# Loading the third tile of x through GpSimd's queue instead of SyncE's

## The chip, the cores and the metric

The kernel runs on one core of a Trainium2 chip. The metric is the device time of one execution in microseconds (us), the median of several runs. Beside it there is one profiled execution, whose trace gives every instruction's start and duration from the first instruction on; its span is the time from the first to the last instruction.

## What is computed

The input is a sequence of 2048 tokens with 512 features, in bf16. It is normalised, then put through a linear-attention block with 32 heads of 16 features and through a gated feed-forward block of width 1792; both results and the input are added.

```
def _A_ref(x, wqkv, w_phi, wo):
    ...
    pq = jnp.einsum("bhsd,hdf->bhsf", q, w_phi)
    pk = jnp.einsum("bhsd,hdf->bhsf", k, w_phi)
    phi_q = jnp.concatenate([_softmax(pq, axis=-1), _softmax(-pq, axis=-1)], axis=-1)
    phi_k = jnp.concatenate([_softmax(pk, axis=-1), _softmax(-pk, axis=-1)], axis=-1)
    kv = jnp.einsum("bhsf,bhsd->bhfd", phi_k, v)
    z  = jnp.einsum("bhsf->bhf", phi_k)
    num = jnp.einsum("bhqf,bhfd->bhqd", phi_q, kv)
    den = jnp.einsum("bhqf,bhf->bhq", phi_q, z)[..., None] + 1e-6
    o = num / den
    ...
def _B_ref(x, w_gate, w_up, w_down):
    g = jnp.einsum("bsd,df->bsf", x, w_gate)
    u = jnp.einsum("bsd,df->bsf", x, w_up)
    h = g * u
    return jnp.einsum("bsf,fd->bsd", h, w_down)
x = A_x
xn = _layernorm(x, axis=-1)
return x + _A_ref(xn, A_wqkv, A_w_phi, A_wo) + _B_ref(xn, B_w_gate, B_w_up, B_w_down)
```

## The kernel before

Tokens are cut into 16 tiles of 128 rows (`NT`), grouped by four (`GT`); a tile of x is 128 x 512 bf16, 128 KB, and lies in `xall[:, n, :]`. It is called x0 to x15 here. Features are cut into four chunks of 128 (`DC`). `xnT` holds the normalised x with the features on the partitions, as matmuls need it.

All weights stay in SBUF. They and x are fetched at the start by a list of DMAs, most of them issued by SyncE one after another (lines 82 to 95): x0, x2, the v part of `wqkv` in two halves (`wv`, L75), then the first columns of the gate and up weights (`wg`, `wu`, L72), `wphi` (L87), more of `wg` and `wu`, the transposed load of the k part (`wT2`, which the trace calls wT, L89), x4 to x7, the rest of `wg` and `wu`, x8 to x15, `wd` and `wo`. x1 and x3 are issued by ScalarE (lines 102 and 103). The issue of every x load stands in the helper `dma_x`, so that it has line 69 in the trace, whichever queue it goes to. GpSimd issues no DMA.

From line 98 on the order of each engine's instructions is that in which they are written (`manual_schedule`). What stands ahead of that line is only the DMAs of SyncE.

The opening treats the first four tiles apart, since nothing else can run before they are in. For a tile n:

- the rows are summed into `tots[n]`: x0 and x3 by VectorE (`sum_of`, L373), x1 and x2 by ScalarE (L377, which writes the scaled copy `junk` and takes the sum from the accumulator);
- VectorE subtracts the sum from 512 times x (`sub_sum`, L337) into `xns[n]`; the missing factor 1/std is put in later, where the results of matmuls are read;
- TensorE transposes the four chunks with the identity `ident` into PSUM (`lt`, L205), and ScalarE, for half of x0 VectorE, copies them to `xnT` (L206);
- TensorE multiplies with `wv` (`first_v` through `proj`, L236), the two first chunks of features for x0, x1 and x2, then the others; the results for x0 and x1 lie in the banks called kv, those of x2 and x3 in banks called pv.

The written order on ScalarE is: sum of x1, sum of x2, then the copies of the transposes. On VectorE: sum of x0, centring of x0 in two halves, centring of x1, copy of half of x0's transposes, centring of x2, sum of x3, centring of x3, then the statistics of all four (L153). On TensorE: eleven warm-up matmuls on a constant (L308; ten before everything else, one after the transposes of x1), transposes of x0 and x1, transposes of x2, v matmuls for x0, x1 and x2, transposes of x3, more v matmuls, then gate and up matmuls (`ffn`, L274 and L278).

GpSimd first makes the constants: `ident` (through `make_identity`, which the trace shows under masks.py:197 and 199), and `BO`, a block mask (L116, L110, L112). Later it computes 1/std (L345, L347), the block diagonal `bd` from `BO` and `wphi` (L212) and, in the main part, the products of the feature maps.

Behind the opening a long part follows in which TensorE goes from one matmul to the next: gate and up matmuls interleaved with the k and v projections of the remaining tiles, then attention and the output matmuls (`fin`, L290 and L293) with the stores.

Of the kernel before, what the change touches and what calls it, by code (L numbers as in the profile page):

```python
# [8 lines left out]
BF16 = mybir.dt.bfloat16  # L9
F32 = mybir.dt.float32  # L10
AF = mybir.ActivationFunctionType
# [10 lines left out]
def kernel(  # L22
# [12 lines left out]
    nc = tc.nc  # L35
    P = 128
    S, D = A_x.shape[-2], A_x.shape[-1]
# [4 lines left out]
    DC = D // P  # L42
# [10 lines left out]
    consts = ctx.enter_context(tc.tile_pool(name="consts", bufs=1))  # L53
# [4 lines left out]
    wv = wpool.tile([P, DC, D], BF16)  # L58
# [9 lines left out]
    def dma_x(lo, hi, eng=nc.sync):  # L68
        eng.dma_start(out=xall[:, lo:hi, :], in_=x_view[:, lo:hi, :])
# [1 line left out]
    def dma_cols(eng, w, src, lo, hi, at=0):  # L71
        eng.dma_start(out=w[:, :, lo - at:hi - at], in_=src[:, lo:hi].rearrange("(c p) f -> p c f", p=P))  # L72

    def dma_wv(lo, hi):
        nc.sync.dma_start(out=wv[:, lo:hi, :],  # L75
                          in_=A_wqkv[lo * P:hi * P, 2 * D:3 * D].rearrange("(c p) f -> p c f", p=P))

    def dma_gu(lo, hi):
        dma_cols(nc.sync, wg, B_w_gate, lo, hi)
        dma_cols(nc.sync, wu, B_w_up, lo, hi)  # L80

    dma_x(0, 1)
    dma_x(2, 3)
    dma_wv(0, 2)
    dma_wv(2, DC)
    dma_gu(0, 2 * P)
    nc.sync.dma_start(out=wphi[:], in_=A_w_phi.rearrange("(c h) d f -> (h d) c f", c=DC))  # L87
    dma_gu(2 * P, 5 * P)
# [5 lines left out]
    nc.sync.dma_start(out=wd[:], in_=B_w_down.rearrange("(c p) d -> p c d", p=P))  # L94
    nc.sync.dma_start(out=wo[:], in_=A_wo.rearrange("(c p) n -> p c n", p=P))

    ET = mybir.EngineType
    ctx.enter_context(tc.manual_schedule(engines={ET.PE, ET.DVE, ET.Activation, ET.Pool, ET.SP}))
    ones = nc.const_aps.tensor(1.0, [P, P], BF16)
    first = consts.tile([P, 1], BF16)  # L100
    nc.scalar.activation(out=first[:], in_=ones[:, 0:1], func=AF.Exp, scale=1.0)
    dma_x(1, 2, nc.scalar)
    dma_x(3, 4, nc.scalar)
    ident = consts.tile([P, P], BF16)
    make_identity(nc, ident[:])
    mhalf = consts.tile([P, GT], F32)
# [416 lines left out]
```

## Time and profile before

| what | us |
|---|---|
| median of 3 runs (lowest, highest) | 220.69 (220.66, 221.0) |
| the profiled execution | 220.62 |
| its span, first to last instruction | 218.9 |
| the two x issues of SyncE, from 0.79 | 0.87 |
| the two x issues of ScalarE, from 0.85 | 0.86 |
| the two wv issues of SyncE, from 1.71 | 0.94 |
| sum of x0 on VectorE starts | 3.36 |
| sum of x1 on ScalarE starts | 3.61 |
| sum of x2 on ScalarE starts | 4.37 |
| transposes of x2 on TensorE start | 5.55 |
| first v matmul starts | 5.79 |

The engines are called PE (TensorE's matmuls), PEld (its weight loads), DVE (VectorE), ACT (ScalarE), POOL (GpSimd) and SP (SyncE); SPq and ACTq are the queues in which they issue DMAs. L69 is line 69 of the kernel; an arrow in a row points from what is read to what is written. The chain of waits is followed back from the last instruction to what released each step. The time that a DMA takes stands as "us to landing", from the start of its issue; it can be several times the duration of the issue itself, which is what a queue's row in the timeline shows. The granted clock of TensorE is 1.0 over the whole span.

### The profile page before, as it was taken

The numbers are of one execution on the slowest core, as the hardware profiler recorded it, in microseconds if no ns is written. First come the engines' busy times: TensorE is split into PE (matmuls) and PEld (weight loads), VectorE is DVE, ScalarE is ACT, GpSimd is POOL, SyncE is SP. The second block draws the span as 40 slices with busy tenths as digits, with TensorE's granted clock in tenths as the row PEclk, the third lists the DMA queues.
The fourth block names the chain that finished last, engine by engine and source line by source line (L and its number), as shares of the span: only waits on it lengthen the run. The fifth ranks groups of instructions, "written<-read, shape, count | busy, mean of one in ns | idle before, by whom it ended". The sixth has DMA issues, their size and how long they took to land.

```text
span 218.9 us, 3494 instructions
## 1 busy us (share of the span) xinstructions
PE 214.9 (98%) x1293; PEld 103.1 (47%) x1293; DVE 140.6 (64%) x239; ACT 89.8 (41%) x160; POOL 74.1 (34%) x71
## 2 busy tenths in 40 slices
PE   7999999999999999999999999999999999999994
PEld 3444445454444444444544444444444444454443
DVE  4868867886598758576599773296655655454321
ACT  6645686569575875565435212141231322100000
POOL 2540843363358554636045333033123033000000
PEclk9999999999999999999999999999999999999999
DMA  6999996003202540202028455114441431612301
GB/s 200 273 301 374 372 235 111 15 0 51 48 0 49 51 91 5 48 3 48 1 41 103 77 114 114 39 24 96 96 75 24 95 72 27 97 48 72 75 24 48
DMA packets 48529, 19.91 MB, mean 91 GB/s; under 512 B 37504, under 2 KB 48512, under 8 KB 48512
## 3 DMA queue, kind: packets, MB, share of 16 engines
q1 hardware_dynamic: 48224, 19.42, 39.7%
q10 hardware_dynamic: 288, 0.26, 0.3%
q8 instruction: 10, 0.16, 0.3%
q14 instruction: 7, 0.06, 0.1%
HBM read 8.67 MB, written 2.10 MB: 49 GB/s over the span
## 4 chain that ended last, share of the span: by engine, by line
PE 96%; DMA 1%; ACT 1%; DVE 0%; issue 0%
PE g L274 22%; PE fin L290 22%; PE u L278 22%; PE fin L293 6%; PE k L236 6%; PE q L236 6%; PE pv L236 6%; PE kv L330 2%; PE ab L462 2%; DMA xall<-in_A_x_dram 1%; PE kv L236 1%; ACT junk L377 1%; PE pq L225 1%; PE tp L205 0%; DVE xn L337 0%; DVE o_sb L300 0%
## 5 line engine op out<-in xcount | busy, mean ns | idle before, releaser
L274 PE MATMUL g<-xnT,wg 128*128 128x512 bf16 x224 | 57.5, 379 | 0.0
L278 PE MATMUL u<-xnT,wu 128*128 128x512 bf16 x224 | 57.5, 379 | 0.0
L282 DVE TENSOR_TENSOR hT<-u,g_sb 128x512 bf16<-128x512 f32 x56 | 37.0, 667 | 24.3 <-PE u L278 16.2
L253 POOL TENSOR_TENSOR phiq<-e,rsum 128x1024 bf16<-128x1024 f32 x16 | 30.9, 1933 | 63.5 <-DVE rsum L251 56.0
L281 ACT CAST g_sb<-g 128x512 bf16<-128x512 f32 x56 | 32.9, 587 | 47.1 <-PE g L274 46.9
L249 DVE TENSOR_REDUCE sums<-e 128x64 f32<-128x1024 f32 x32 | 38.9, 1216 | 20.1 <-ACT e L246 20.1
L290 PE MATMUL fin<-wd,hT 128*128 128x512 bf16 (+2 forms) x238 | 51.1, 366 | 0.0
L253 POOL TENSOR_TENSOR phik<-e,rsum 128x1024 bf16<-128x1024 f32 x16 | 30.9, 1932 | 40.0 <-DVE rsum L251 37.9
L278 PEld LDWEIGHTS <-wu 128*128 128x128 bf16 x224 | 21.9, 98 | 26.4
L290 PEld LDWEIGHTS <-hT 128*128 128x128 bf16 x238 | 22.5, 98 | 24.7
L274 PEld LDWEIGHTS <-wg 128*128 128x128 bf16 x224 | 21.1, 98 | 24.0
L236 PEld LDWEIGHTS <-xnT 128*128 128x128 bf16 x192 | 17.5, 98 | 18.3 <-ACT xnT L206 0.3
L300 DVE TENSOR_TENSOR o_sb<-fin,xall 128x512 bf16<-128x512 f32 (+2 forms) x13 | 8.5, 651 | 20.5 <-PE fin L293 20.5
L251 DVE RECIPROCAL rsum<-sums 128x64 f32<-128x64 f32 x32 | 17.7, 553 | 3.1
L293 PE MATMUL fin<-wo,oT 128*128 128x512 bf16 (+2 forms) x68 | 16.6, 366 | 0.0
L236 PE MATMUL k<-W1k,xnT 128*128 128x512 bf16 x64 | 16.4, 379 | 0.0
L236 PE MATMUL q<-W1q,xnT 128*128 128x512 bf16 x64 | 16.4, 378 | 0.0
L245 ACT ACTIVATE e<-q 128x512 f32<-128x512 f32 x12 | 7.2, 597 | 22.2 <-PE q L236 22.2
L236 PE MATMUL pv<-wv,xnT 128*128 128x512 bf16 x56 | 14.4, 379 | 0.0
L475 DVE TENSOR_TENSOR otok<-ab,rden 128x512 bf16<-128x512 f32 x16 | 11.1, 692 | 0.6
L322 ACT CAST vt<-pv 128x512 bf16<-128x512 f32 x12 | 7.0, 587 | 10.0 <-PE pv L236 10.0
L153 DVE BATCH_NORM_STATS2 stats<-xall 128x6 f32<-128x512 bf16 x16 | 10.6, 665 | 0.0
(62 smaller groups left out, 130.6 us busy)
## 6 DMA issues: line engine op xcount, KB each, us to landing
out_dram<-o_sb SPq DMA_DIRECT2D x15, 128.0 KB, 2.0
wd<-in_B_w_down_dram SPq DMA_DIRECT2D x1, 1792.0 KB, 15.5
xall<-in_A_x_dram SPq DMA_DIRECT2D x1, 1024.0 KB, 11.4
wg<-in_B_w_gate_dram SPq DMA_DIRECT2D x1, 640.0 KB, 8.5
wu<-in_B_w_up_dram SPq DMA_DIRECT2D x1, 640.0 KB, 9.7
wv<-in_A_wqkv_dram SPq DMA_DIRECT2D x2, 256.0 KB, 4.1
xall<-in_A_x_dram SPq DMA_DIRECT2D x1, 512.0 KB, 4.3
wg<-in_B_w_gate_dram SPq DMA_DIRECT2D x1, 512.0 KB, 5.2
```

The source lines that it names most:

```text
L153: nc.vector.bn_stats(out=stats[:], in_=xall[:, n, :])
L236: nc.tensor.matmul(ps, lhsT=xnT[:, j, n * P:(n + 1) * P], rhs=w[:, j, :], start=(j == 0), stop=(j == DC - 1))
L249: nc.vector.tensor_reduce(out=sums[:], in_=ev, axis=AX.X, op=ALU.add)
L251: nc.vector.reciprocal(out=rsum[:].rearrange("p a b -> p (a b)"), in_=sums[:])
L253: nc.gpsimd.tensor_tensor(out=phi[:].rearrange("p g (x f) -> p (g x) f", f=DH), in0=ev, in1=rsum[:].to_broadcast((P, 2 * H, DH)), op=ALU.mult)
L274: nc.tensor.matmul(gps, lhsT=wg[:, c, f * P:(f + 1) * P], rhs=xnT[:, c, T * TT:(T + 1) * TT], start=(c == 0), stop=(c == DC - 1))
L278: nc.tensor.matmul(ups, lhsT=wu[:, c, f * P:(f + 1) * P], rhs=xnT[:, c, T * TT:(T + 1) * TT], start=(c == 0), stop=(c == DC - 1))
L281: nc.scalar.copy(out=g_sb[:], in_=gps)
L282: nc.vector.tensor_tensor(out=hTs[T][:, f, :], in0=ups, in1=g_sb[:], op=ALU.mult)
L290: nc.tensor.matmul(ps, lhsT=hTs[T][:, f, t4 * P:(t4 + 1) * P], rhs=wd[:, f, lo:lo + w], start=(f == 0), stop=False)
L293: nc.tensor.matmul(ps, lhsT=oTs[n][:, c, :], rhs=wo[:, c, lo:lo + w], start=False, stop=(c == DC - 1))
L475: nc.vector.tensor_tensor(out=o_tok[:].rearrange("p (b h d) -> p b h d", b=2, d=DH), in0=abv[:, :, :, 0:DH], in1=rden[:].to_broadcast((P, ...
```

## The change

x2 goes to GpSimd's queue; SyncE issues x0 and then wv in its two halves, followed by the unchanged rest of its list; ScalarE issues x1 and x3 as before. In the text the block with `manual_schedule`, the first activation and ScalarE's two loads moves up ahead of SyncE's remaining DMAs, so that these now stand behind the line from which the written order is kept. GpSimd's load of x2 stands ahead of `make_identity` and `BO`, so it is GpSimd's first instruction behind the four small constants that every program starts with. `dma_wv` takes the issuing engine as an argument, and gets SyncE both times.

```
-    def dma_wv(lo, hi):
-        nc.sync.dma_start(out=wv[:, lo:hi, :],
-                          in_=A_wqkv[lo * P:hi * P, 2 * D:3 * D].rearrange("(c p) f -> p c f", p=P))
+    def dma_wv(lo, hi, eng):
+        eng.dma_start(out=wv[:, lo:hi, :],
+                      in_=A_wqkv[lo * P:hi * P, 2 * D:3 * D].rearrange("(c p) f -> p c f", p=P))
...
     dma_x(0, 1)
-    dma_x(2, 3)
-    dma_wv(0, 2)
-    dma_wv(2, DC)
+    dma_wv(0, 2, nc.sync)
+    dma_wv(2, DC, nc.sync)
+
+    ET = mybir.EngineType
+    ctx.enter_context(tc.manual_schedule(engines={ET.PE, ET.DVE, ET.Activation, ET.Pool, ET.SP}))
+    ones = nc.const_aps.tensor(1.0, [P, P], BF16)
+    first = consts.tile([P, 1], BF16)
+    nc.scalar.activation(out=first[:], in_=ones[:, 0:1], func=AF.Exp, scale=1.0)
+    dma_x(1, 2, nc.scalar)
+    dma_x(3, 4, nc.scalar)
+    dma_x(2, 3, nc.gpsimd)
     dma_gu(0, 2 * P)
     nc.sync.dma_start(out=wphi[:], in_=A_w_phi.rearrange("(c h) d f -> (h d) c f", c=DC))
     dma_gu(2 * P, 5 * P)
...
-    ET = mybir.EngineType
-    ctx.enter_context(tc.manual_schedule(engines={ET.PE, ET.DVE, ET.Activation, ET.Pool, ET.SP}))
-    ones = nc.const_aps.tensor(1.0, [P, P], BF16)
-    first = consts.tile([P, 1], BF16)
-    nc.scalar.activation(out=first[:], in_=ones[:, 0:1], func=AF.Exp, scale=1.0)
-    dma_x(1, 2, nc.scalar)
-    dma_x(3, 4, nc.scalar)
     ident = consts.tile([P, P], BF16)
     make_identity(nc, ident[:])
```

## The prediction

> **What bounds the kernel now.** First the busy shares and the chain that ended last.
>
> ```profile
> span 218.9 us, 3494 instructions
> ...
> PE 214.9 (98%) x1293; PEld 103.1 (47%) x1293; DVE 140.6 (64%) x239; ACT 89.8 (41%) x160; POOL 74.1 (34%) x71
> ...
> PE 96%; DMA 1%; ACT 1%; DVE 0%; issue 0%
> ```
>
> TensorE is busy for 214.9 of 218.9 us. The 4.0 us without it lie in three places by the timeline: 0.83 before its first warm-up matmul, 0.28 between the last of these (ends 4.14) and the first transpose at 4.42, and 2.86 after its last matmul (215.80 + 0.24 = 216.04), while the last tile is added and stored. From 4.42 to 216.04 TensorE has no hole. So a change of loads can move the end only through the first 5.6 us, and what it moves there is passed on whole: nothing later can absorb it. That stretch of the chain of waits reads:
>
> ```profile
> 0.85 2.74 DMA xall<-in_A_x_dram
> 3.59 0.02 issue
> 3.61 0.46 ACT junk L377
> 4.07 0.08 issue
> 4.15 0.19 ACT junk L377
> 4.34 0.02 issue
> 4.37 0.73 ACT junk L377 x2
> 5.10 0.05 issue
> 5.15 0.36 DVE xn L337
> 5.51 0.05 issue
> 5.55 0.40 PE tp L205 x4
> 5.95 0.86 PE kv L236 x4
> ```
>
> Columns are start, length, what. x1 (issued by ScalarE at 0.85) lands at 3.59; ScalarE sums its rows (L377) until 4.34, sums x2 from 4.37 to 5.10, VectorE centres x2 (L337), TensorE transposes it at 5.55, and the v matmuls follow without a hole. x2's load is not in this chain: ScalarE is not ready for it before 4.37. When it lands comes from the loads that were in flight at 1.17 and at 1.27 us.
>
> ```profile
> xall<-in_A_x_dram SPq DMA_DIRECT2D x1, 128.0 KB, 2.5
> xall<-in_A_x_dram ACTq DMA_DIRECT2D x1, 128.0 KB, 2.7
> ...
> xall<-in_A_x_dram SPq DMA_DIRECT2D x1, 128.0 KB, 2.8
> xall<-in_A_x_dram ACTq DMA_DIRECT2D x1, 128.0 KB, 3.1
> ```
>
> The last figure is us from issue to landing: x0, x1, then x2 and x3. x2's issue begins between 1.235 and 1.255, so it lands at about 1.25 + 2.8 = 4.05, which is 0.32 before its use. x3's begins between 1.255 and 1.275: 1.27 + 3.1 = 4.37, used at 5.41 (L373).
>
> **The change part by part.** *SyncE loses one issue.* Its two x issues take 0.87 us together, with the step to the next one 0.92, so everything behind moves up by about 0.46. wv's halves land at 1.71 + 3.9 = 5.61 and about 2.2 + 4.2 = 6.4 now, and would land about 0.46 sooner. Neither is waited for: the first kv matmul (5.79) comes straight behind the transposes of x2, the second half is first read at 7.31. The first pieces of wg and wu land at 2.69 + 4.6 = 7.3 and 3.20 + 5.2 = 8.4, used at 9.46 and 10.33; wphi at 3.75 + 4.8 = 8.55, used at 12.27; wT at 6.28 + 6.3 = 12.6, used at 14.74. All are early now, so earlier is worth 0. Part of the 0.46 is lost anyway, or kept, at one wait of SyncE's own, 0.8 us until wv's first half has landed, which holds the second piece of wu at 5.62; that piece lands at 10.9 and is read at 13.57.
>
> *GpSimd gains one issue, ahead of all its constants.* Behind it stand the identity (done at 1.35, read by the transposes at 4.42) and BO (done at 2.40, read at 12.27); then GpSimd idles 4.99 us until 7.39. An issue of up to 3.07 us costs nothing there; beyond that the identity would be late.
>
> ```profile
> 0.78 0.20 POOL masks.py:197 MEMSET ident<- 128x128 bf16 x1 [0.29 <-POOLq L507]
> 1.06 0.29 POOL masks.py:199 TENSOR_SCALAR_AFFINE_SELECT ident<-ident 128x128 bf16<-128x128 bf16 x1
> ```
>
> *ScalarE* keeps its order: table, x1, x3. The statement that fixes the written order adds no instruction.
>
> *x2 itself* is the one price that no row shows, since no load goes through GpSimd's queue here. It can be issued at 0.78 instead of 1.25. From below: as fast as the fastest x tile, 2.5, it lands at 3.28 and costs 0. From above: as slow as the slowest small load of the opening, wphi's 16 KB with 4.8, it lands at 5.58, 1.23 us too late with the 0.02 that ScalarE takes after a landing. I take a value between. GpSimd spends 1.08 us on its one instruction over a 128x512 bf16 tile (bd, L212), and I give the issue that, against 0.42 for ScalarE's issues (0.86 for two, the single ones 0.38 and 0.46). After its issue x3 needed 3.1 - 0.42 = 2.68 more, in the same crowd of loads: 0.78 + 1.08 + 2.68 = 4.54. Then the share: the transfer engines are full from 2.4 to 4.0 (336, 318, 366 and 312 GB/s in the four stretches of 0.4, DMA share 0.94 to 1.10). x2 shared them with x3 alone; now wv, x3 and x2 come from three queues. 128 KB at 333 GB/s take 0.39; one more such share for half of the time is 0.20. Landing 4.74, start of the sum 4.76 instead of 4.37: late by 0.39.
>
> The Trainium skill speaks for less, and for a gain that ends there: in "DMA: Bandwidth & Descriptors", section "Latency and other measured facts", the first byte comes after about 1 us from GpSimd and about 0.6 us from SyncE or ScalarE. By that 0.4, put on x2's own 2.8, it would land at 0.78 + 3.2 = 3.98 and cost nothing; no run here shows it yet.
>
> Late by 0.39, x2's sum holds up on ScalarE the copies of x0's and x1's transposes (L206, from 5.00), which the first v matmuls read, and on VectorE the centring of x2 and all of x3's part; TensorE waits at the transposes of x2 with nothing to fill in. The whole 0.39 reaches the end. The profiled execution took 220.62 (218.9 of span and 1.7 around it), so 221.01 by it; it lies 0.07 under the median of the runs, and 220.69 + 0.39 = **221.1 us**.
>
> **The rivals.** *A, hidden:* x2 lands by 4.35 and nothing changes, 220.7. For it: the issue starts 0.47 earlier, and x2 has 0.32 of room now, so GpSimd's way may be slower than SyncE's by 0.77 before it shows. Against: the extra issue time (0.66) and share (0.20) of my sum come to 0.86. The skill's 0.4 from above belongs to this rival.
>
> *B, much slower:* the queue is used for the first time at the very start, and its load behaves like wphi's row, at the far end: 1.23 late, 221.9. It is over 0.2% once x2 lands after 4.79, and a case of its own from 0.9 late. For it: loads of the opening take 4.6 to 5.2 once the queues are full. Against: those were issued from 2.69 on, behind others, and x2 would come at 0.78, when nothing is in flight.
>
> *C, faster:* x1 no longer has x2 for company and lands as x0 does, 2.5 after issue, at 3.35 instead of 3.59; with x2 in time the chain gains up to 0.24, 220.45. Against: wv's first half takes x2's place behind x0 on SyncE's queue at the same moment, and VectorE is itself busy until about 5.15 (its copy, L206, starts at 4.94), so most of the gain would be lost to it. Beyond 0.24 only a change in the 1.7 us outside the span could go.
>
> **How the numbers follow.** The forecast, late by 0.1 to 0.9 (220.8 to 221.6), has 0.55; A 0.21; B 0.17; C 0.07. A measurement of this kernel tells about 0.2%, 0.44 us, from no change. The forecast's interval is split by that nearly in the middle: 0.27 within, 0.28 beyond. Slower: 0.28 + 0.17 = 0.45. Same: 0.27 + 0.21 and 0.02 of C = 0.50. Faster: the rest of C, 0.05. The range runs from C's end, rounded, to B's end, rounded: 220.5 to 222.0; outside lie most of C and the cases worse than wphi's row, some 0.15.
>
> **What would show it.** A GpSimd issue of x2 near 0.78 with its time to landing: 3.96 by my sum, 3.57 or less for A, 4.8 for B. ScalarE's second sum (L377) starting at 4.76 with x2's load as its releaser; the transposes of x2 at 5.94 instead of 5.55, and a hole of that size on TensorE ahead of them; the identity still done long before 4.42. If the second sum starts at 4.37 and the time still moves, the cause is another. If x1 lands later than 3.59 because x2 shares with it, the first sum moves instead of the second: the price would be mine, its place not.

## The result, and the profile after

| | us |
|---|---|
| before, median of 11 runs (lowest, highest) | 221.0 (220.65, 221.16) |
| changed, median of 11 runs (lowest, highest) | 221.92 (221.74, 223.44) |
| ratio, 95% interval | 1.0064 [1.0049, 1.008] |
| the profiled execution before and after | 220.62, 221.74 |
| its span before and after | 218.9, 220.0 |

The change makes the kernel slower by about 0.9 us in the median. The ratio is that of the means, 1.4 us, which four of the eleven runs, at 222.5 to 223.4, pull up. The page of the changed kernel shows a new queue, and the share of DMA in the chain has grown from 1 to 2%:

```profile
span 220.0 us, 3471 instructions
...
q0 software_dynamic: 48, 0.13, 0.1%
...
PE 95%; DMA 2%; issue 1%; ACT 0%; DVE 0%; POOLq 0%; ACTq 0%
```

The queue q0 is GpSimd's: it moves x2's 0.13 MB in 48 packets, where ScalarE's queue takes 288 for two tiles. The chain of waits over the first 8 us (start, length, what) says where the time went:

```profile
0.69 0.61 issue
1.29 0.00 POOLq masks.py:199
1.29 4.16 DMA xall<-in_A_x_dram
5.45 0.02 issue
5.47 0.02 ACTq L378
5.49 0.05 issue
5.54 0.73 ACT junk L378 x2
6.27 0.03 issue
6.29 0.37 DVE xn L338
6.66 0.05 issue
6.71 0.40 PE tp L206 x4
7.10 0.86 PE kv L237 x4
```

All lines of the changed kernel are one higher than before. x1 has left the chain; x2's load through GpSimd stands in it, from 1.29 to 5.45. The second sum on ScalarE starts at 5.54 instead of 4.37, the transposes of x2 at 6.71 instead of 5.55, and the span is 1.1 longer: all of the lateness reaches the end. TensorE stands idle for 1.25 us ahead of these transposes, as the last figure of their row in the timeline says:

```profile
6.71 0.40 PE L206 MATMUL tp<-ident,xn 128*128 128x128 bf16 x4 [1.25 <-DVE xn L338]
```

The loads in flight about 1.27 us, with us to landing as the last figure, and GpSimd's first instructions in the timeline:

```profile
wv<-in_A_wqkv_dram SPq DMA_DIRECT2D x1, 256.0 KB, 3.9
xall<-in_A_x_dram ACTq DMA_DIRECT2D x1, 128.0 KB, 3.8
xall<-in_A_x_dram POOLq DMA_DIRECT2D x1, 128.0 KB, 4.2
```
```profile
1.29 0.77 POOL L69 DMA_DIRECT2D xall<-in_A_x_dram  x1 [0.80 <-POOLq L508]
2.06 0.22 POOL masks.py:197 MEMSET ident<- 128x128 bf16 x1
2.36 0.29 POOL masks.py:199 TENSOR_SCALAR_AFFINE_SELECT ident<-ident 128x128 bf16<-128x128 bf16 x1
```

Two things besides x2's 4.2 are to be seen. The issue starts at 1.29, half a microsecond after the other queues' first issues, and takes 0.77. And x3, still ScalarE's second load, lands 3.8 after the start of its issue instead of 3.1. The identity is done at 2.65, well ahead of its use at 4.39.

### The profile page after: what moved, and what is told of

It is laid out like the page before. It is cut to its first block, busy times and chain, and to the rows that moved or that the text cites. A ratio compares the mean times of both kernels' runs of the same rounds, so it can differ in the third digit from the quotient of the medians.

```text
span 220.0 us, 3471 instructions
## 1 busy us (share of the span) xinstructions
PE 213.6 (97%) x1269; PEld 103.1 (47%) x1293; DVE 140.7 (64%) x239; ACT 89.7 (41%) x160; POOL 74.9 (34%) x72
## 4 chain that ended last, share of the span: by engine, by line
PE 95%; DMA 2%; issue 1%; ACT 0%; DVE 0%; POOLq 0%; ACTq 0%
PE g L275 22%; PE u L279 22%; PE fin L291 22%; PE fin L294 6%; PE q L237 6%; PE k L237 6%; PE pv L237 5%; PE ab L463 2%; DMA xall<-in_A_x_dram 2%; PE kv L331 2%; PE kv L237 1%; PE pq L226 1%; ACT junk L378 0%; PE tp L206 0%; DVE xn L338 0%
## 5 line engine op out<-in xcount | busy, mean ns | idle before, releaser
L275 PE MATMUL g<-xnT,wg 128*128 128x512 bf16 x215 | 56.5, 379 | 0.5
L279 PE MATMUL u<-xnT,wu 128*128 128x512 bf16 x220 | 56.8, 379 | 0.2
L237 PE MATMUL k<-W1k,xnT 128*128 128x512 bf16 x60 | 15.7, 379 | 0.1
```

The lines of the kernel that those rows point to most:

```text
L237: nc.tensor.matmul(ps, lhsT=xnT[:, j, n * P:(n + 1) * P], rhs=w[:, j, :], start=(j == 0), stop=(j == DC - 1))
L275: nc.tensor.matmul(gps, lhsT=wg[:, c, f * P:(f + 1) * P], rhs=xnT[:, c, T * TT:(T + 1) * TT], start=(c == 0), stop=(c == DC - 1))
L279: nc.tensor.matmul(ups, lhsT=wu[:, c, f * P:(f + 1) * P], rhs=xnT[:, c, T * TT:(T + 1) * TT], start=(c == 0), stop=(c == DC - 1))
```

## The experiments

Twelve experiments ran, one of them the changed kernel once more. Unless said otherwise an edit is against the changed kernel, and a time stands against the median of the kernel before, run on the same chip in the same series. Each has one profiled execution, so a landing read from a trace is that of one execution, and the other runs can differ.

### The moved block alone

```
     dma_x(0, 1)
+    dma_x(2, 3)
...
-    dma_x(2, 3, nc.gpsimd)
```

> The changed kernel with x2 put back on SyncE's queue behind x0, so that only the moved block of statements is left of the change. Theory (the whole loss is x2's late landing through GpSimd's queue): the time of the kernel before, 221.0 within 0.3 us; the second sum on ScalarE starts near 4.37. Rival (the moved block, with the order of SyncE's loads now fixed by hand, or the order in which completions are awaited, costs something): about 221.9.

Measured: 220.86 against 220.92, ratio 0.9999 [0.999, 1.0008]. In the profiled execution the second sum starts at 4.26, x2's transposes at 5.54, the span is 218.9. The moved statements cost nothing; the whole loss goes with the queues.

### x1 through GpSimd

```
-    dma_x(1, 2, nc.scalar)
+    dma_x(2, 3, nc.scalar)
     dma_x(3, 4, nc.scalar)
-    dma_x(2, 3, nc.gpsimd)
+    dma_x(1, 2, nc.gpsimd)
```

> x1 goes through GpSimd's queue, ScalarE's queue takes x2 and x3. Theory: x1 lands near 5.45 and its sum, the first of ScalarE's two, starts there instead of at 3.61, late by 1.85; the second follows 0.76 later, and the whole delay reaches the end: 221.0 + 1.85 = 222.85. Rival (a fixed cost of having a load in that queue, the same for every tile): 221.9, as with x2.

Measured: 222.47 against 220.92, ratio 1.0094 [1.0064, 1.0123]. The chain of waits of this kernel:

```profile
1.29 3.78 DMA xall<-in_A_x_dram
5.06 0.02 issue
5.09 0.03 ACT junk L378
...
5.84 0.73 ACT junk L378 x2
```

x1 landed at 5.06 and its sum started at 5.09 instead of 3.61, late by 1.48; the second sum followed at 5.84 instead of 4.37. The price is the lateness against the first use (1.48 in the trace, 1.55 in the medians). With four runs, from 222.04 to 223.81, the times alone do not rule out the same price for every tile; the kernels with x3 in that queue, further down, do. The size of 1.85 was missed because the load was quicker in this trace: 3.78 from issue to landing instead of 4.16.

### x3 through GpSimd, x2 as ScalarE's second load

```
-    dma_x(3, 4, nc.scalar)
-    dma_x(2, 3, nc.gpsimd)
+    dma_x(2, 3, nc.scalar)
+    dma_x(3, 4, nc.gpsimd)
```

> x3 instead of x2 goes through GpSimd's queue, ScalarE's queue takes x1 and x2. Theory (what counts is the landing against the first use): x3 lands near 5.45 as x2 did, its sum on VectorE started at 5.41 before, and the transposes of x3 have 0.4 us of room on TensorE, so the time is that of the kernel before, 221.0 within 0.3. x2 is then ScalarE's second load, lands near 4.37 as x3 did before, and its sum starts at 4.4. Rival (any load in GpSimd's queue at the start costs about 1 us, by holding up the other loads or GpSimd itself): 221.9.

Measured: 221.23 against 220.92, ratio 1.0033 [1.001, 1.0056]; neither number. The reason is not x3 (its 4.4 from issue to landing ends at 5.7, its sum starts at 6.33 behind x2's), but x2, which ScalarE's own queue brought late:

```profile
1.27 3.95 DMA xall<-in_A_x_dram
5.22 0.02 issue
5.24 0.02 ACTq L378
5.26 0.05 issue
5.31 0.73 ACT junk L378 x2
```

Two changes stood beside this load: wv, now directly behind x0 on SyncE's queue, and the load on GpSimd's. The next two kernels part them.

### No load through GpSimd, wv in its new place

```
+    dma_x(2, 3, nc.scalar)
     dma_x(3, 4, nc.scalar)
-    dma_x(2, 3, nc.gpsimd)
```

> No load through GpSimd: SyncE issues x0 and then wv as in the changed kernel, ScalarE x1, x2 and x3. In the kernel with x3 on GpSimd's queue, x2 as ScalarE's second load landed at 5.22 in place of the 4.37 that x3 had there before. Theory W (wv's first half, moved up to the place right behind x0, holds up ScalarE's second load): x2 lands near 5.2 here too, and the time is 221.2 to 221.6. Theory G (GpSimd's issue held it up): x2 lands near 4.4, and the time is 220.9 to 221.1.

Measured: 221.05 against 221.04, ratio 1.0013 [0.9996, 1.003]. In its chain x2's load takes 3.37:

```profile
1.26 3.37 DMA xall<-in_A_x_dram
4.63 0.02 issue
4.65 0.02 ACTq L378
4.67 0.05 issue
4.72 0.73 ACT junk L378 x2
```

x2 landed at 4.63: 0.26 later than x3 in the same slot before, not 0.85. That is nearer to theory G, as is the time. So wv's move alone holds up ScalarE's second load a little. That a load in GpSimd's queue holds it up further is not certain: with both, ScalarE's second load took between 3.4 and 4.2 over seven profiles, and the 3.4 here lies at the edge of that. For the time the 0.34 of this profile does not stand out of the spread of the kernel before (220.63 to 221.65 in this series).

ScalarE's third load, x3, issued behind x2, is the last row of the loads issued between 1.72 and 1.80 us:

```profile
xall<-in_A_x_dram ACTq DMA_DIRECT2D x1, 128.0 KB, 4.6
```

It took as long as a load through GpSimd's queue. The three issues of ScalarE end at 2.19, so x3 landed some 4.1 after the end of its own; x2, whose issue ended at 1.71, needed 2.9. In the changed kernel GpSimd's issue of x2 ends at 2.06, and the landing comes 3.39 behind it. So in this profile the load that was handed over last waited longest, on ScalarE's queue too.

### x4 in SyncE's second place, wv at its old time

```
     dma_x(0, 1)
+    dma_x(4, 5)
...
-    dma_x(4, 8)
+    dma_x(5, 8)
```

> The changed kernel with a load of x4 (128 KB) in SyncE's second place, where x2 stood before, so that wv and all behind it keep their old times; x2 still goes through GpSimd's queue. If GpSimd's queue alone makes x2 late: x2 lands at 5.2 to 5.5, the time stays at 221.7 to 221.9. If wv's move made it late: x2 lands by 4.6, 221.1. x3 on ScalarE's queue lands near 4.4 again by theory W, at 5.05 as in the changed kernel by theory G.

Measured: 222.04 against 221.04, ratio 1.0053 [1.0034, 1.0071]. In the profiled execution x2 landed 5.14 after 1.29, at 6.43, later still than expected, and x3 on ScalarE's queue at 1.27 + 3.3 = 4.57. So x2 is late without wv's move too; x3's 3.3, between the 3.1 of before and the 3.8 of the changed kernel, is nearer to theory W. The fifth tile in flight (x4, in the place that x2 had) is part of this crowd, so the kernel does not show GpSimd's queue alone. Nor did x2's packets start later here than in the changed kernel: the first stand between 3.2 and 3.6 us, 40 of the 48 in GpSimd's queue had moved by 4.8 us, and the landing waited for the last eight, the last of them between 6.0 and 6.4. This execution was the longest of its runs, 224.53, with a span 3.9 over that of before, of which x2's transposes (7.69 instead of 5.55) explain 2.14. Four other runs lie at 221.3 to 221.6, only 0.3 to 0.6 above the kernel before, so x2 cannot have been this late in them. The rest of the 3.9 is TensorE's clock, which is the last figure but two of each row of the windows:

```profile
8.00:9.00 1.00, 1.00 (x7) 0.35 (x5) 0.96 (x3) 0.58 (x1) 0.00 (x0) 0.79 1.07 286
9.00:10.00 1.00, 1.00 (x5) 0.45 (x4) 0.97 (x3) 0.00 (x0) 0.39 (x2) 0.50 1.10 342
10.00:11.00 1.00, 1.00 (x7) 0.55 (x5) 0.93 (x5) 0.51 (x1) 0.83 (x3) 0.50 1.83 264
11.00:12.00 1.00, 1.00 (x4) 0.35 (x3) 0.78 (x3) 0.07 (x1) 0.83 (x3) 0.50 0.64 56
12.00:13.00 1.00, 1.00 (x6) 0.47 (x5) 0.75 (x1) 0.33 (x1) 0.83 (x3) 1.00 1.27 289
```

After the hole ahead of x2's transposes the granted clock is 0.79, 0.50, 0.50, 0.50 for a microsecond each: 0.21 + 3 x 0.50 = 1.71 us of work are lost.

### x2 alone in flight

```
-    dma_x(0, 1)
-    dma_wv(0, 2, nc.sync)
-    dma_wv(2, DC, nc.sync)
...
+    dma_x(2, 3, nc.gpsimd)
+    hold = consts.tile([P, 2, 16], BF16)
+    nc.sync.dma_start(out=hold[:, 0, :], in_=xall[:, 2, 0:16])
+    dma_x(0, 1)
+    dma_wv(0, 2, nc.sync)
+    dma_wv(2, DC, nc.sync)
+    nc.scalar.dma_start(out=hold[:, 1, :], in_=xall[:, 2, 16:32])
     dma_x(1, 2, nc.scalar)
     dma_x(3, 4, nc.scalar)
-    dma_x(2, 3, nc.gpsimd)
```

> Every other load of the opening waits until x2 has landed through GpSimd's queue (SyncE and ScalarE first issue a tiny copy that reads x2), so the time itself is worth nothing here, some 5 us more. If the lateness of x2 is the queue's own latency: issue at 1.29, landing at 4.8 to 5.3. If it is the crowd of the other loads: landing near 3.8, that is, issue 0.77 and then about 1.7.

Measured in its chain of waits:

```profile
1.29 2.46 DMA xall<-in_A_x_dram
3.75 0.02 issue
3.77 0.54 SPq L89
```

Without other loads x2 lands at 3.75, 0.6 ahead of its use. The queue's own latency is not what made it late. The same is seen in the packets of q0 in the list of queues (packets, MB, share of the 16 engines), here from 2.4 to 2.8 and from 2.8 to 3.2 us:

```profile
q0 software_dynamic: 6, 0.02, 27.1%
...
q0 software_dynamic: 24, 0.09, 78.5%
```

and in the changed kernel, from 4.0 to 4.4 and from 4.4 to 4.8 us; ahead of 4.0 there are none:

```profile
q0 software_dynamic: 18, 0.07, 44.9%
...
q0 software_dynamic: 23, 0.05, 33.7%
```

In finer windows the first packets start between 2.7 and 2.8 us here and between 4.1 and 4.2 in the changed kernel: the same issue at the same moment has its first packets about 1.4 us later when the other queues are full. That is most of the 1.70 between the two landings; the rest is that the packets are spread wider. The Trainium skill, page "DMA: Bandwidth & Descriptors", section "Latency and other measured facts", has the first byte about 1 us after the issue from GpSimd. With nothing else in flight the first packets came 1.4 to 1.5 after the issue's start, in the changed kernel 2.8 to 2.9 after it, and the measurement decides.

### Only the tiles of x in flight

```
-    dma_wv(0, 2, nc.sync)
-    dma_wv(2, DC, nc.sync)
...
     dma_x(2, 3, nc.gpsimd)
+    hold = consts.tile([P, 16], BF16)
+    nc.sync.dma_start(out=hold[:], in_=xall[:, 2, 0:16])
+    dma_wv(0, 2, nc.sync)
+    dma_wv(2, DC, nc.sync)
```

> SyncE issues x0 and then waits for x2 (by a tiny copy that reads it) before wv and all other weights, so that only x0, x1 and x3 are in flight beside x2's load through GpSimd's queue; wv is late and the time is worth nothing. With no other load x2 landed 2.46 us after its start at 1.29, with all of them 4.16 after it. If the stream of weights behind x0 holds x2 up: landing 2.5 to 3.1 after the start, at 4.4 or sooner. If the three tiles of x are enough to do it: 3.5 or more after the start, at 4.8 or later.

Measured: x2 landed 3.55 after 1.29, at 4.84. So x0, x1 and x3 alone, which land by 4.1 in this kernel, are enough to bring x2 past its use at 4.37. The 0.6 between this and the 5.45 of the changed kernel goes with the weights, as far as one profile of each can tell.

### x0 and x2 on SyncE, x3 through GpSimd

```
     dma_x(0, 1)
+    dma_x(2, 3)
...
-    dma_x(3, 4, nc.scalar)
-    dma_x(2, 3, nc.gpsimd)
+    dma_x(3, 4, nc.gpsimd)
```

> SyncE issues x0, x2 and then wv as in the kernel before, ScalarE x1 alone, GpSimd x3. Theory (GpSimd's queue has a latency of its own at the start, the first packets at about 4.0 and the landing at 5.1 to 5.5, whatever else is in flight): x3 lands just about when its sum starts (5.4), x2 lands at 4.05 or sooner, and the time is that of the kernel before, 220.9 within 0.3. Rival (wv's earlier place in the changed kernel is what made x2 late, and GpSimd's queue is as quick as the others once wv stands behind): x3 lands by 4.5, the same time. Second rival (a load in GpSimd's queue costs time by itself): 221.5 or more.

Measured: 221.12 against 221.04, ratio 1.0012 [0.9998, 1.0026]. x3 took 4.1 and landed at 5.4, its sum started at 5.46. With the tile that is used last in that queue, and wv in its old place, the same lateness is free. It is no faster than before either. The queue's latency "whatever else is in flight", on which the expectation rested, is refuted by the kernel with x2 alone, and by this one too: its first packets in GpSimd's queue start between 3.1 and 3.2, not at 4.0.

### The identity ahead of the load

```
-    dma_x(2, 3, nc.gpsimd)
...
     make_identity(nc, ident[:])
+    dma_x(2, 3, nc.gpsimd)
```

> GpSimd makes the identity first and then issues x2. The issue stood at 1.29 in the changed kernel, 0.5 after the engines start at 0.8. If that half microsecond is work of GpSimd's sequencer on the load's instruction, it goes on beside the identity's two instructions (0.78 to 1.35): the issue starts at 1.3 to 1.5, x2 lands as in the changed kernel, time 221.9 within 0.4. If it is a time from the start before which the queue does not run, the issue also starts by 1.5. If it is spent in order, after whatever stands before it: the issue starts at 1.85, x2 lands 0.5 later, 222.4.

Measured: 224.98 against 221.18, ratio 1.0174 [1.0147, 1.0201]. The start behaved as the first reading has it: the identity's two instructions run from 0.79 to 1.36 and the issue starts at 1.47, 0.18 later than without them. The time is far off all three expectations, because the landing is:

```profile
1.36 0.11 issue
1.47 5.87 DMA xall<-in_A_x_dram
```

With a start 0.18 later came a landing 1.9 later. As with x4 in second place, it waited for the last packets: the first of q0 start between 4.0 and 4.4 and 37 of the 48 move by 5.2, but some still run after 6.8. The hole on TensorE is 3.2 us, and the halved clock follows in the profiled execution. All four runs, from 224.44 to 225.41, are this long. When x2 lands among the other loads is thus not a fixed time.

### TensorE's hole filled: six and four warm-up matmuls

```
-        warm_up(1)
+        warm_up(6)
```

> The changed kernel with six warm-up matmuls instead of one ahead of the transposes of x2: about 1.1 us more of TensorE work in the hole of 1.25 us. Theory: TensorE waits for x2 all the same, so the lower runs stay at 221.8 to 221.9. Four of the changed kernel's eleven runs lie at 222.5 to 223.4; if these are runs in which TensorE's clock falls back after the hole, they vanish here and the highest run is below 222.4; if they are runs in which x2 lands still later, they stay.

Measured: 221.79 against 220.92, ratio 1.0039 [1.0025, 1.0053]; eight runs from 221.35 to 222.2. No run lies above 222.4, as the reading by the clock has it; the lower runs, three of them at 221.35 to 221.5, lie below the 221.8 that was expected. In the profiled execution the six ran until 7.34 and were themselves the last thing ahead of the transposes, so four were tried, beside the changed kernel itself.

```
-        warm_up(1)
+        warm_up(4)
```

> The changed kernel with four warm-up matmuls instead of one in TensorE's hole, 0.65 us more of work, which end before x2's transposes can start. Theory (the runs far above the others are runs in which TensorE's clock is halved for some 3.4 us after the hole, as in the trace with x4 in SyncE's second place): median 221.7 to 221.9, set by x2's landing, and no run above 222.5. Rival (they are runs in which x2 lands later still): runs above 222.5 as often as in the changed kernel itself, which runs beside it.

> The changed kernel itself once more, for a second profile and more runs beside the one above: 221.9 in the median, some runs in four above 222.5. Its second sum on ScalarE starts again more than 0.5 us after 4.37, as late as x2 lands, and the excess of the span over 218.9 is that lateness, plus about 1.7 if the profiled execution has TensorE's clock at half for 3.4 us.

Measured, against 221.26: with four, 221.72, ratio 1.0029 [1.0015, 1.0044], the highest of twelve runs 222.9 and the next 222.16, and six of the twelve below 221.70; the changed kernel itself 221.92, ratio 1.0048 [1.0026, 1.007], with three of twelve runs at 223.2 to 224.0 and the lowest at 221.70. One run with four lies above the bound that was set, so the expectation was missed by that one. Why the lower runs gain as well stays open. Over both series 7 of 23 runs of the changed kernel lie above 222.5, and 1 of 20 of the filled ones; of the kernel before, no run of any series is above 221.82. But such runs are not the changed kernel's alone: the kernel with x3 through GpSimd and x2 on ScalarE has two in twelve, at 223.46 and 223.49, and that with no load through GpSimd one in eleven, at 223.22. The second profile of the changed kernel shows one such run. It took 223.58; x2 landed at 1.29 + 4.32 = 5.61, and the windows read:

```profile
7.00:8.00 1.00, 1.00 (x7) 0.46 (x6) 0.96 (x3) 0.76 (x2) 0.00 (x0) 0.58 1.20 254
8.00:9.00 1.00, 1.00 (x4) 0.36 (x3) 0.96 (x3) 0.00 (x0) 0.21 (x2) 0.50 1.11 326
9.00:10.00 1.00, 1.00 (x6) 0.55 (x5) 0.95 (x3) 0.00 (x0) 0.83 (x3) 0.50 1.31 300
10.00:11.00 1.00, 1.00 (x7) 0.49 (x5) 0.94 (x3) 0.59 (x1) 0.83 (x3) 0.71 1.15 201
```

0.42 + 0.50 + 0.50 + 0.29 = 1.71 us lost to the clock.

Whether the other six are such runs is not shown. A loss of 1.71 in 222 makes a mean granted clock of 0.992; that is listed for three of the seven, this one among them, and 0.999 to 1.0 for the other four. But the listed clock does not catch every slow stretch. In the kernel with x2 alone in flight TensorE stands idle from 4.30 to 8.52, and the first four kv matmuls then take nearly twice as long as in the kernel before, while the clock in the windows stays at 1.00. The first row is of that kernel, the second of the kernel before:

```profile
10.23 1.91 PE L239 MATMUL kv<-wv,xnT 128*128 128x512 bf16 x4
```
```profile
5.79 1.03 PE L236 MATMUL kv<-wv,xnT 128*128 128x512 bf16 x4
```

So in those four runs either the clock fell unlisted or x2 landed still later, as it does in the kernel with the identity first; no trace shows which. That 1 of 20 filled runs is so long, against 7 of 23, speaks for the clock without deciding it.

### The account over the profiles

Lateness is the start of x2's transposes less the 5.55 of before; the excess is the span less 218.9. The two kernels that hold the other loads back are left out.

| kernel | lateness | clock loss | excess |
|---|---|---|---|
| the moved block alone | 0.0 | 0 | 0.0 |
| x3 last, through GpSimd | 0.08 | 0 | 0.3 |
| no load through GpSimd | 0.34 | 0 | 0.4 |
| x3 through GpSimd, x2 on ScalarE | 0.92 | 0 | 0.9 |
| four warm-ups | 0.98 | 0 | 1.0 |
| changed, first profile | 1.16 | 0 | 1.1 |
| x1 through GpSimd | 1.46 | 0 | 1.4 |
| six warm-ups | 1.63 | 0 | 1.6 |
| changed, second profile | 1.32 | 1.71 | 3.0 |
| x4 in second place | 2.14 | 1.71 | 3.9 |
| identity first | 3.05 | 1.53 | 4.5 |

In the last row the clock was at half from 8.24 to 11.66, but TensorE's work began at 8.60, so only (11.66 - 8.60) / 2 = 1.53 is lost. In the row "x3 last" no load is late: its first matmuls were slow (the eight transposes of x0 and x1 took 1.07 instead of 0.85, the warm-up matmul behind them 0.63 instead of 0.38), so that the first v matmul starts at 6.09 instead of 5.79. The profiled execution before, 220.62, lies 0.38 under the median of its runs, so these excesses stand above what the medians show.

## Why the prediction was right or wrong

The time lies in the stated range, and the place is as foreseen: x2's landing takes the place of x1's in the chain, ScalarE's second sum waits for it, TensorE waits at x2's transposes with nothing to do, and nothing later absorbs it. The size was wrong, a loss of 0.92 in the medians and a lateness of 1.17 in the trace instead of 0.39. The step that failed is the price of x2's landing, "0.78 + 1.08 + 2.68 = 4.54" with a share of "0.20" on top:

- *The start, 0.78.* It was 1.29: 0.51 too early. The prediction took the moment at which GpSimd began the identity. Most of the half microsecond goes on beside other instructions of GpSimd (with the identity first the issue starts 0.11 after it), but here only the four constants stood before the load.
- *The issue, 1.08.* It was 0.77, 0.31 less.
- *From the issue's end to the landing, 2.68 + 0.20.* It was 3.39, 0.51 more. Alone in flight it is 1.69 (2.46 less 0.77), so the other loads cost 1.70. The prediction took ScalarE's x3 of the kernel before as the measure, "in the same crowd of loads", and added a share. But the crowd did not stay the same: wv's first half, 256 KB, had moved up to the second place. In the changed kernel x3 itself needed 3.8 - 0.42 = 3.38 after its issue instead of 2.68, as much as x2's 3.39. In this profile, then, GpSimd's load fared no worse behind its issue than ScalarE's beside it; the measure was right and its value was that of another crowd. Over the kernels here the others' delay of a load through GpSimd's queue lies between 1.3 and 3.4 us (landings 3.8 to 5.9 after the start, with all the loads in flight, against 2.46 alone). The far end, in the kernels with x4 in second place and with the identity first, is beyond what ScalarE's x3 met there (3.3 and 3.5 from issue to landing).

The sum of the three, 0.51 - 0.31 + 0.51 = 0.71, is the difference between 4.74 and 5.45.

*SyncE's loads earlier are worth 0.* Right for what SyncE loads: the first v matmuls still come straight behind x2's transposes. What was not priced is that wv's new place holds up ScalarE's second load: x3 by 0.7 here (3.1 to 3.8), x2 in that slot by 0.26 where nothing goes through GpSimd's queue. It was covered, because its use had moved to 6.57; in the kernel with x2 in that slot it decided the time.

*The identity* stayed covered, as written. *ScalarE keeps its order* and *the moved statement adds no instruction* held: the moved block alone costs nothing.

Of the rivals, *A, hidden* fell with the landing at 5.45; the 0.4 on which it drew (the Trainium skill, "DMA: Bandwidth & Descriptors", section "Latency and other measured facts") leaves out what the other loads add, 1.70 here. *B, much slower* gave the number, 221.9, and had 0.17; that wphi's row ends so near is luck, as nothing ties a 16 KB load issued at 3.75 to this one. Its argument was half right: the price came from the opening's crowd, and the argument held against it, that x2 would come when nothing is in flight, failed because its first packets move at 4.1. It named the queue's first use as the reason, and that is not borne out: a first use with nothing else in flight is quick. *C* was not seen; its share had been split wrongly, since a gain of up to 0.24 ends at 220.45, nearly all of it inside the range that begins at 220.5, and none of it the 0.44 away from no change that the prediction itself asks for.

Not foreseen at all is the second way in which the hole costs: in 7 of 23 runs of the changed kernel the time is above 222.5, and in the one of them with a trace TensorE's clock is halved after the hole. For the other six it is not shown. These runs set the upper end and raise the mean, not the median.

What stays open is how the other loads delay GpSimd's queue: whether its packets wait for a turn at the transfer engines or for something that must be fetched before them. The runs show that the delay needs other loads in flight and that it varies; they do not show the mechanism. One regularity bears on it. The first packets in GpSimd's queue start the later, the more the other queues had been handed before its issue: at 2.7 with nothing, at 3.1 (x3 last) and 3.3 (only the tiles) behind three tiles of x, at 3.6 behind four (x4 in second place), at 3.9 to 4.2 behind three tiles and wv's first half, the size of five. At the 312 to 366 GB/s of the full engines 128 KB take 0.36 to 0.42. That fits a load that waits its turn behind what was issued before it, but no run varies this alone, and it does not explain the last packets that were late in two kernels.

## What to carry to other kernels

A queue that has never been used in a kernel has no row to price it by, and the rows of the other queues in the kernel before are no upper bound, since the change itself alters the crowd (x3, on an unchanged queue, went from 3.1 to 3.8): give such a queue the load that is used last (x3 here, free), not the one that is used third. Before moving a load to shorten a queue, look whether anything waits for what stands behind it; here nothing did, and so there was nothing to gain. And a hole of about a microsecond early in a TensorE-bound kernel can cost more than itself, when the clock falls back behind it: 1.71 in the one trace of the changed kernel that has it.

## What the runs showed of the hardware that was not expected

- One 128 KB load through GpSimd's queue took 2.46 us from its issue with nothing else in flight, 3.55 beside three tiles of x, and 3.78 to 5.87 among all the loads of the opening. In one kernel it started 0.18 us later and landed 1.9 later. Loads of the same size on ScalarE's queue took 3.0 to 4.2 as the second in it, and 4.6 as the third.
- The load's issue on GpSimd started at 1.29 as the first instruction behind the four constants, when other engines started at 0.79, and at 1.47 behind two instructions that take from 0.79 to 1.36: most of the 0.5 runs beside them.
- The granted clock fell to 0.5 for about 3.4 us after a hole of 1.25 us (5.62 to 6.87, with 0.45 idle shortly before it), at a cost of 1.7. In the first profile a hole of the same 1.25 us left it at 1.0, and the four kv matmuls behind it took 1.03 as in the kernel before. The Trainium skill, page "TensorE: Matmul & The Clock Gate", section "Part 1: The HAM clock gate (the "warmup" mystery)", has the clock fall after an idle window of about 3.4 us that runs free of the kernel; the time at half clock agrees with such a window, the hole that was enough is shorter.
- The listed clock of 1.0 is not proof of full speed: behind an idle stretch of 4.2 us four kv matmuls took 1.91 instead of 1.03 with the clock at 1.00 in the windows, and in the kernel before the warm-up matmuls take 0.63 each in the median, also at a listed 1.00, where the one behind x1's transposes takes 0.38.
